# Projecting the keys of a linear attention in two 64-row tiles, by token parity

## The chip, the cores and the metric

The kernel runs on one core of one Trainium2 chip. The metric is the device time of one execution in microseconds, and for a kernel the median of its runs. Three runs before the change gave 900.4, 898.79 and 900.29 us: the median is 900.29 us. The engines are named as in the profile: PE (TensorE) for matmuls and PEld for its weight loads, DVE (VectorE), ACT (ScalarE), POOL (GpSimd), and SP, which issues most of the loads and stores.

## The reference

Three stages follow one another, all in float32. The first is an attention with features, for 4 batches, 8 heads, 576 tokens, 64 numbers per head and 128 features:

```python
def phi(x):
    proj = np.einsum('bhsd,df->bhsf', x, w_phi)
    proj = proj - np.max(np.abs(proj), axis=-1, keepdims=True)
    return np.concatenate([np.exp(proj), np.exp(-proj)], axis=-1)
q_p, k_p = (phi(q), phi(k))
kv = np.einsum('bhsf,bhsd->bhfd', k_p, v)
z = np.sum(k_p, axis=2)
num = np.einsum('bhsf,bhfd->bhsd', q_p, kv)
den = np.einsum('bhsf,bhf->bhs', q_p, z)[..., None] + 1e-06
```

Its result `num / den`, as 2304 rows of 512, goes through `((x @ w1) * (x @ w2)) @ w3 @ w_out`, and that through `g @ w_out` with `g = relu(x @ w_in)**2`.

## The kernel before

The attention works on pairs of heads: 16 pairs, four to a batch. Of a pair's 576 tokens, 512 are handled as four blocks of 128 (`C = 4`, `P = 128`), and the 64 left over, the tail, together with the tail of the next pair. Even pairs carry the work for the tails of two pairs, odd pairs don't, so that the pattern repeats after a double slot: an even and an odd pair.

For each pair PE transposes q and k into PSUM (`turn_q`, `turn_k`, line 350, tiles `pqt` and `pkt`; `turn_tails` makes `ptt`). Each transposed block is split into a high and a low part (`high_part`, line 353 on ACT; `low_part`, line 356 on DVE) with the tiles `qT`, `kT`, `tT`. Every product of two such values is made of three matmuls, high by high, low by high, high by low. The queries are projected by `project_sides` (line 436) into `pq`; the keys by `proj_k` (line 312), with a block of `kT` as the stationary operand and `wbd`, the feature weights of both heads in a block-diagonal layout, as the moving one. `project_k` is called for j = 0 and 1 (two PSUM banks `pk`, two token blocks each) and j = 2 (the tail). From `pk` DVE takes the largest absolute value (`peak_k`, line 411, tile `kmax`) and subtracts it (`less_k`, line 421, tile `kp`); ACT makes both exponentials (`exp_k`, line 428). `values` (line 511) multiplies them with v, `tail_values` (line 521) adds the tail; ACT copies the sum to `kv` (`keep_values`, line 529). For the queries, `max_q` and `max_qt` (line 451) find the maxima, `max_rows` (line 459) transposes them, `max_parts` (lines 466 to 469, tile `mh`) splits them, `send` moves them through a DMA into `mrow`, and `minus_q` (line 483) subtracts them in PSUM; then `exp_q` follows. One pair later `out` (lines 543 and 551) multiplies queries with `kv`, `keep` (line 559, tile `nd`) copies the result, `reciprocals` and `quotients` divide (DVE line 566, POOL line 578, tile `xd`); two pairs later `turn_x` (line 584) transposes the finished rows, and `keep_x` stores them.

Between these steps the weights of the first MLP are loaded and decoded (`w-1`, `w0`, `w1` and so on: a load on SP, `dy_...` on ACT at line 150, `dt_...` on DVE, additions on POOL).

The order of all this is written out by hand in four tables. `START` covers the first pairs and `END` the last ones from slot 13 on; in between a loop walks through `SLOT` for even and `ODD` for odd slots. An entry as `project_k0/5` runs a step for slot 5; each step has an offset, so that for slot t `turn_k` works on pair t + 1, `project_k` on pair t, `out` on pair t - 1 and `turn_x` on pair t - 2. The order of the entries is the order of the instructions on every engine: each engine works its own queue off in that order, and waits where an operand or a buffer is not ready. Of PSUM, three banks rotate (tag `t`) among `pkt`, `pqt`, `ptt`, the `pk` and `pkv`; `pq` and `po` are single.

Behind the attention, from about 188 us on, come the MLPs, which the change doesn't touch.

## Time and profile before

| what | value |
|---|---|
| median of three runs | 900.29 us |
| the profiled execution, its own time | 902.77 us |
| its span in the profile | 901.0 us |
| granted clock, mean over the span | 0.998 |
| PE busy | 887.2 us, 98% |
| PE weight loads busy | 773.6 us |
| DVE busy | 569.9 us, 63% |
| ACT busy | 412.1 us, 46% |
| POOL busy | 147.4 us, 16% |

Shares are of the whole span. Of the attention, some 188 us, the windows of 20 us show DVE and ACT much busier than that, at 15 to 17 us of 20 each, beside a PE of 18 to 20. Positions in the trace are microseconds from the start of the span. The profiled execution is one of its own and is 2.5 us above the median.

### The profile page before, as it was taken

What the parts mean: (1) busy time and instruction counts of PE and PEld (TensorE: products, weight loads), DVE (VectorE), ACT (ScalarE), POOL (GpSimd) and SP (SyncE); (2) the same over time, 40 slices, a digit from 0 to 9 for tenths busy, and PEclk for the clock granted to TensorE, in tenths of its full rate; (3) what the DMA queues carried; (4) which work ended last, traced back from release to release, by engine and by line L of the source; (5) the groups of instructions that cost most, each with busy time, mean ns of one, the idle gap of its engine ahead of it and who ended that gap; (6) DMA issues with size and microseconds to landing.
All of it is one profiled execution on the core that took longest, in us unless ns stands there. A gap on an engine that the chain in (4) does not pass through costs nothing.

```text
span 901.0 us, 16482 instructions
## 1 busy us (share of the span) xinstructions
PE 887.2 (98%) x6468; PEld 773.6 (86%) x6468; DVE 569.9 (63%) x1070; ACT 412.1 (46%) x787; POOL 147.4 (16%) x130
## 2 busy tenths in 40 slices
PE   8999999999999999999999999999999999999998
PEld 6888888778888888998888898989898998989896
DVE  6877777656766476567887865465745347643533
ACT  5888877754544545555565422232422123322211
POOL 3555655444212440000000000000000000000000
PEclk9999999999999999999999999999999999999999
DMA  6456565557343355758887898577586664684621
GB/s 172 138 164 179 149 189 162 136 131 172 94 140 94 118 164 164 260 167 293 298 289 281 312 398 317 176 269 256 176 315 204 246 227 148 236 325 157 227 99 71
DMA packets 120238, 182.72 MB, mean 203 GB/s; under 512 B 60320, under 2 KB 79584, under 8 KB 120160
## 3 DMA queue, kind: packets, MB, share of 16 engines
q1 hardware_dynamic: 119104, 180.84, 60.6%
q8 instruction: 51, 0.84, 0.4%
q10 hardware_dynamic: 1056, 0.82, 0.3%
q14 instruction: 27, 0.22, 0.1%
HBM read 140.54 MB, written 40.89 MB: 201 GB/s over the span
## 4 chain that ended last, share of the span: by engine, by line
PE 86%; ACT 4%; DMA 3%; DVE 3%; issue 1%; SPq 1%; POOL 1%; DVEq 0%; POOLq 0%; ACTq 0%
PE op L1319 22%; PE yp L1026 11%; PE pa L248 11%; PE pb L248 11%; PE ph_y L1283 8%; PE ph_x L1283 6%; PE ph_w L1283 6%; PE pf L953 5%; ACT kp L428 2%; DMA raw_w<-in_moe_w_dram 2%; PE pkv L511 1%; PE pq L436 1%; PE pk L312 1%; PE po L543 1%; ACT qp L490 1%
## 5 line engine op out<-in xcount | busy, mean ns | idle before, releaser
L1319 PE MATMUL op<-pair,r 128*128 128x512 f32 x864 | 202.9, 391 | 0.0
L1319 PEld LDWEIGHTS op<-pair,r 128*128 128x128 f32 x864 | 161.8, 188 | 32.2
L1026 PE MATMUL yp<-g,w3o 128*128 128x512 f32 (+1 forms) x480 | 105.1, 368 | 0.0
L1026 PEld LDWEIGHTS yp<-g,w3o 128*128 128x128 f32 x480 | 84.2, 189 | 14.9
L248 PE MATMUL pa<-c,w_w12a 128*128 128x512 f32 (+1 forms) x432 | 93.6, 366 | 0.0
L248 PE MATMUL pb<-c,w_w12b 128*128 128x512 f32 (+1 forms) x432 | 93.5, 366 | 0.0
L1283 PE MATMUL ph_y<-yf_t,pair 128*128 128x384 f32 x432 | 86.9, 335 | 0.0
L248 PEld LDWEIGHTS pa<-c,w_w12a 128*128 128x128 f32 x432 | 75.2, 189 | 13.1
L248 PEld LDWEIGHTS pb<-c,w_w12b 128*128 128x128 f32 x432 | 75.2, 189 | 13.1
L1283 PEld LDWEIGHTS ph_y<-yf_t,pair 128*128 128x128 f32 x432 | 76.1, 188 | 0.8 <-issue 0.4
L1370 DVE TENSOR_TENSOR u<-ph_y,m 128x384 f32<-128x384 f32 x24 | 13.4, 558 | 73.5 <-PE ph_y L1283 72.3
L1193 ACT ACTIVATE g<-g 128x512 fp32r<-128x512 f32 (+1 forms) x39 | 23.0, 590 | 78.4 <-DVE g L1191 78.4
L1283 PE MATMUL ph_x<-yf_b,pair 128*128 128x384 f32 x288 | 58.2, 337 | 0.0
L1191 DVE TENSOR_TENSOR g<-pb,a 128x512 f32<-128x512 f32 (+1 forms) x39 | 24.8, 636 | 51.9 <-PE pb L248 51.8
L1296 ACT ACTIVATE r<-m 128x384 fp32r<-128x384 f32 x43 | 22.6, 526 | 73.6 <-DVE m L1295 73.6
L1283 PEld LDWEIGHTS ph_x<-yf_b,pair 128*128 128x128 f32 x288 | 51.3, 188 | 1.9
L428 ACT ACTIVATE kp<-kp 128x512 f32<-128x512 f32 (+1 forms) x80 | 46.6, 589 | 7.6 <-DVE kp L421 6.2
L1366 ACT COPY m<-ph_x 128x384 f32<-128x384 f32 x24 | 11.5, 481 | 74.2 <-PE ph_x L1283 74.2
L953 PE MATMUL pf<-w_wo,w3T 128*128 128x512 f32 x192 | 45.0, 390 | 0.0
L953 PEld LDWEIGHTS pf<-w_wo,w3T 128*128 128x128 f32 x192 | 36.0, 188 | 7.5
L1297 DVE TENSOR_TENSOR r<-m,r 128x384 fp32r<-128x384 f32 x43 | 24.0, 558 | 25.4 <-ACT r L1296 25.4
L511 PEld LDWEIGHTS pkv<-vs,kp 128*64 128x64 f32 x1024 | 34.0, 143 | 6.4 <-ACT kp L428 3.4
(181 smaller groups left out, 1515.0 us busy)
## 6 DMA issues: line engine op xcount, KB each, us to landing
pair<-pair_hbm SPq DMA_DIRECT2D x144, 512.0 KB
pair_hbm<-w_w SPq DMA_DIRECT2D x32, 512.0 KB
raw_w<-in_moe_w_in_dram SPq DMA_DIRECT2D x16, 512.0 KB
raw_w<-in_moe_w_out_dram SPq DMA_DIRECT2D x16, 512.0 KB
pair_hbm<-v_w SPq DMA_DIRECT2D x16, 512.0 KB
raw_w<-in_moe_w_dram SPq DMA_DIRECT2D x56, 128.0 KB
x<-x_hbm SPq DMA_DIRECT2D x12, 512.0 KB
yi<-y_hbm SPq DMA_DIRECT2D x12, 384.0 KB
```

The source lines that it names most:

```text
L248: nc.tensor.matmul(ps[:, 0:n], a, c, start=kk + i == 0, stop=kk == KD - 1 and i == 2)
L428: nc.scalar.activation(z["kp", j][:, :, s, :], z["kp", j][:, :, 1, :], AF.Exp, scale=1.0 - 2.0 * s)
L511: nc.tensor.matmul(z["pkv"][h, s, j], z["kp", j][:, c, s, h], z["vs"][:, j, c, :], start=j + s + c == 0, stop=False, skip_group_check=True,)
L953: nc.tensor.matmul(pf, a, c, start=n == 0, stop=n == len(todo) - 1)
L1026: nc.tensor.matmul(blk.yp[i][:, 0:blk.n], a, d, start=c == blk.c0 and s == 0, stop=c == blk.c1 - 1 and s == 2)
L1191: nc.vector.tensor_tensor(out=g32[:, 0:n], in0=pb[:, 0:n], in1=a_sb[:, 0:n], op=ALU.mult)
L1193: nc.scalar.activation(g[:, 0, 0:n], g32[:, 0:n], AF.Copy)
L1283: nc.tensor.matmul(ps_, a, c, start=start and n == 0, stop=n == 5, skip_group_check=not start)
L1296: nc.scalar.activation(r[:, 0], h, AF.Copy)
L1297: nc.vector.tensor_tensor(out=r[:, 1], in0=h, in1=r[:, 0].bitcast(F32), op=ALU.subtract)
L1319: nc.tensor.matmul(z.ops[i], a, d, start=z.p + j + s == 0, stop=z.p == NP2 - 1 and j == 1 and s == 2)
L1370: nc.vector.tensor_tensor(out=u2, in0=y, in1=m1, op=ALU.add)
```

## The change

The keys are projected in two tiles of 64 rows each. Rows 0 to 63 of a transposed block hold the even tokens of a block of token pairs and rows 64 to 127 the odd ones. Each half is now the stationary operand of a matmul of its own, with the 64-row feature weights `wss` as the moving one, 128 columns in place of the 256 of `wbd`; even tokens go into one PSUM bank, odd tokens into another, and the two alternate from matmul to matmul. So there are 24 matmuls of 128x128 in place of 12 of 128x256 per pair. Both banks are one step, `project_k`; the tail keeps its form (`project_k2`). `peak_k`, `less_k` and `exp_k`, as code, stay as they are, but what 0 and 1 stand for is now the parity of the token and no longer a group of blocks; `values` picks its blocks accordingly, in the same number of matmuls. The four tables are written in another order. The diff of the tables, from which a line or two says little, is cut to its `ODD` part; the functions follow whole:

```diff
 ODD = """
-project_k0 peak_k0 project_q project_qt max_q tail_values< keep_values turn_x w1 keep_x max_qt turn_k w0 max_rows w1
-less_k0 project_k1 max_parts out turn_q peak_k1 high_k exp_k0 less_k1 exp_k1 keep turn_tails low_k values0 reciprocals
...
+project_k project_q project_qt tail_values< peak_k0 max_qt max_q keep_values w1 turn_x keep_x turn_k less_k0 max_rows
+w0 high_k turn_q out w1 max_parts exp_k0 send fetch_q fetch_k w-1 store_x peak_k1 less_k1 exp_k1 keep turn_tails
...
@@ -307,13 +306,6 @@
                 )
             return t
 
-        def proj_k(ps, at, kT, c):
-            for n, (a, b) in enumerate(passes((kT[:, 0], kT[:, 1]), (wbd[:, 0], wbd[:, 1]))):
-                nc.tensor.matmul(
-                    ps[:, at:at + 2 * F], a[:, c * P:(c + 1) * P], b.rearrange("p j f -> p (j f)"),
-                    start=n == 0, stop=n == 2,
-                )
-
         todo = [(b, pr) for b in range(B) for pr in range(NPR)]
         live = [{} for _ in todo]
         tails = {}
@@ -395,13 +387,25 @@
         def low_tail(z):
             low_part(z["tT"], z["ptt"][:, 0:2 * P])
 
-        def project_k(z, j):
-            z["pk", j] = ps = bank(f"pk_{z['nm']}_{j}")
-            if j < 2:
-                for g in range(2):
-                    proj_k(ps, g * 2 * F, z["kT"], 2 * j + g)
-            else:
-                proj_k(ps, 0, z["tT"][:, :, P:], 0)
+        def project_k(z):
+
+            at = [bank(f"pk_{z['nm']}_{u}") for u in range(2)]
+            for i in range(4):
+                for n, (a, b) in enumerate(((0, 0), (0, 1), (1, 0))):
+                    for u in range(2):
+                        h = slice(u * D, (u + 1) * D)
+                        nc.tensor.matmul(
+                            at[u][:, i * F:(i + 1) * F], z["kT"][h, a, i * P:(i + 1) * P], wss[h, b, :],
+                            start=n == 0, stop=n == 2,
+                        )
+            z["pk", 0], z["pk", 1] = at
+
+        def project_k_tails(z):
+            z["pk", 2] = ps = bank(f"pk_{z['nm']}_2")
+            for n, (a, b) in enumerate(passes((z["tT"][:, 0], z["tT"][:, 1]), (wbd[:, 0], wbd[:, 1]))):
+                nc.tensor.matmul(
+                    ps[:, 0:2 * F], a[:, P:], b.rearrange("p j f -> p (j f)"), start=n == 0, stop=n == 2
+                )
 
         def peak_k(z, j):
 
@@ -501,17 +505,18 @@
 
         halves_f = [slice(0, F // 2), slice(F // 2, F)]
 
-        def values(z, j):
-
-            if j == 0:
+        def values(z, u):
+
+            if u == 0:
                 z["pkv"] = bank(f"pkv_{z['nm']}")[:, 0:4 * (D + 1)].rearrange("p (s j d) -> p s j d", s=2, j=2)
-            for s in range(2):
-                for c in range(C):
-                    for h in halves_f:
-                        nc.tensor.matmul(
-                            z["pkv"][h, s, j], z["kp", j][:, c, s, h], z["vs"][:, j, c, :],
-                            start=j + s + c == 0, stop=False, skip_group_check=True,
-                        )
+            for j in range(2):
+                for s in range(2):
+                    for g in range(2):
+                        for h in halves_f:
+                            nc.tensor.matmul(
+                                z["pkv"][h, s, j], z["kp", u][:, 2 * j + g, s, h], z["vs"][:, j, 2 * g + u, :],
+                                start=u + j + s + g == 0, stop=False, skip_group_check=True,
+                            )
 
         def tail_values(z):
             pr = z["pr"]
@@ -708,8 +713,10 @@
         }
         for j in range(2):
             steps[f"values{j}"] = 0, lambda z, j=j: values(z, j)
+        steps["project_k"] = 0, project_k
+        steps["project_k2"] = 0, even(project_k_tails)
         for j in range(3):
-            for name, f in (("project_k", project_k), ("peak_k", peak_k), ("less_k", less_k), ("exp_k", exp_k)):
+            for name, f in (("peak_k", peak_k), ("less_k", less_k), ("exp_k", exp_k)):
                 steps[f"{name}{j}"] = 0, even(f, j) if j == 2 else lambda z, f=f, j=j: f(z, j)
 
 
```

The rows below show how that stands on three engines. `pk_1_0` and `pk_1_1` are the two banks of pair 1 of a batch, `pq_100` the queries, `pq_101` their tail and the row of maxima, `pkv_0` and `vt` the values of the pair before.

PE, the end of an even slot and the odd slot behind it, before:

```order
L511 MATMUL pkv_0_984<-vs_93,kp_0_1_982 64x65 x16
L312 MATMUL pk_1_0_1058<-wbd,kT_1_957 128x256 x6
L436 MATMUL pq_100<-qT_1_1016,wss 128x512 x6
L436 MATMUL pq_101<-tT_0_826,wss 128x128 x3
L521 MATMUL pkv_0_984<-vt_96,kp_0_2_1021 64x130 x4
L584 MATMUL po<-ident,xd_3_1018 128x128 x5
L350 MATMUL pkt_2_1092<-ident,km_2_1012 128x128 x4
L459 MATMUL pq_101<-ident,m_1_98 128x128
L312 MATMUL pk_1_1_1104<-wbd,kT_1_957 128x256 x6
L543 MATMUL po<-kv_0_1081,qp_0_1045 64x65 x32
L350 MATMUL pqt_2_1148<-ident,qm_2_1010 128x128 x4
```

The same place after the change (the two middle rows go on alternating, 24 in all):

```order
L516 MATMUL pkv_0_1061<-vs_93,kp_0_1_1050 64x65 x16
L397 MATMUL pk_1_0_1118<-wss,kT_1_974 128x128
L397 MATMUL pk_1_1_1119<-wss,kT_1_974 128x128
...
L440 MATMUL pq_100<-qT_1_1059,wss 128x512 x6
L440 MATMUL pq_101<-tT_0_871,wss 128x128 x3
L526 MATMUL pkv_0_1061<-vt_96,kp_0_2_1105 64x130 x4
L589 MATMUL po<-ident,xd_3_1099 128x128 x5
L342 MATMUL pkt_2_1171<-ident,km_2_1036 128x128 x4
L463 MATMUL pq_101<-ident,m_1_98 128x128
L342 MATMUL pqt_2_1184<-ident,qm_2_1034 128x128 x4
L548 MATMUL po<-kv_0_1161,qp_0_1102 64x65 x32
```

The second bank of `pk` has moved from behind the transposes of the keys to the front of the slot, ahead of `pq`, and the transposes of the queries (`pqt`) from behind the outputs (`po` from `kv` and `qp`) to ahead of them.

DVE, in an even slot, from the second reduction of the keys on, before:

```order
L411 TENSOR_REDUCE kmax_0_1_970<-pk_0_1_897 128x4
L466 TENSOR_REDUCE mh_0_976<-pq_101 48x32
L468 TENSOR_REDUCE m_0_978<-pq_101 48x32
L469 TENSOR_TENSOR mh_0_976<-m_0_978,mh_0_976 48x32
L356 TENSOR_TENSOR kT_1_957<-pkt_1_912,kT_1_957 128x512
L421 TENSOR_TENSOR kp_0_1_982<-pk_0_1_897,kmax_0_1_970 128x4x128
L566 TENSOR_SCALAR rc_3_1003<-nd_3_974 128x10
L569 RECIPROCAL rc_3_1003<-rc_3_1003 128x10
L411 TENSOR_REDUCE kmax_0_2_1006<-pk_0_2_964 128x2
L421 TENSOR_TENSOR kp_0_2_1021<-pk_0_2_964,kmax_0_2_1006 128x2x128
L152 TENSOR_SCALAR dt_wo_905<-dy_wo_904 128x512
L153 SCALAR_TENSOR_TENSOR dt_wo_905<-raw_wo_823,dt_wo_905 128x512
```

And after:

```order
L470 TENSOR_REDUCE mh_0_1025<-pq_101 48x32
L472 TENSOR_REDUCE m_0_1027<-pq_101 48x32
L473 TENSOR_TENSOR mh_0_1025<-m_0_1027,mh_0_1025 48x32
L415 TENSOR_REDUCE kmax_0_1_1030<-pk_0_1_938 128x4
L348 TENSOR_TENSOR kT_1_974<-pkt_1_967,kT_1_974 128x512
L425 TENSOR_TENSOR kp_0_1_1050<-pk_0_1_938,kmax_0_1_1030 128x4x128
L415 TENSOR_REDUCE kmax_0_2_1054<-pk_0_2_1019 128x2
L571 TENSOR_SCALAR rc_3_1056<-nd_3_1048 128x10
L574 RECIPROCAL rc_3_1056<-rc_3_1056 128x10
L151 TENSOR_SCALAR dt_wo_964<-dy_wo_963 128x512
L152 SCALAR_TENSOR_TENSOR dt_wo_964<-raw_wo_839,dt_wo_964 128x512
L425 TENSOR_TENSOR kp_0_2_1105<-pk_0_2_1019,kmax_0_2_1054 128x2x128
```

The parts of the maxima (`mh`) have moved ahead of the reduction `kmax_0_1`, the tail's reduction `kmax_0_2` ahead of the reciprocals, and the tail's difference `kp_0_2` behind the decoding of a weight.

ACT, at the end of the attention, slot 14 (`dy_w_0` decodes a part of w3, `nd_1` is the copy of the outputs), before:

```order
L173 ACTIVATE w_w12b_2744<-dt_w12b_2591 128x512
L353 ACTIVATE kT_3_2794<-pkt_3_2782 128x512
L150 ACTIVATE dy_w_0_2796<-raw_w_0_2675 128x512
L428 ACTIVATE kp_2_0_2780<-kp_2_0_2780 128x4x128 x2
L559 COPY nd_1_2850<-po 128x650
L428 ACTIVATE kp_2_1_2856<-kp_2_1_2856 128x4x128 x2
L353 ACTIVATE qT_3_2898<-pqt_3_2866 128x512
```

And after:

```order
L345 ACTIVATE kT_3_2973<-pkt_3_2968 128x512
L172 ACTIVATE w_w12b_2896<-dt_w12b_2775 128x512
L432 ACTIVATE kp_2_0_2966<-kp_2_0_2966 128x4x128 x2
L564 COPY nd_1_3027<-po 128x650
L149 ACTIVATE dy_w_0_3033<-raw_w_0_2876 128x512
L432 ACTIVATE kp_2_1_3036<-kp_2_1_3036 128x4x128 x2
L345 ACTIVATE qT_3_3052<-pqt_3_3046 128x512
```

The decoding `dy_w_0` has moved from ahead of the first exponentials and the copy `nd_1` to behind them. At the start of the kernel, likewise, the transposes of the first tail (`turn_tails/-1`) now stand ahead of the first `project_q/0` in the table. On SP the sends and loads keep their order among one another but for the first few; on POOL the order is the same.

## Rows read from the trace of the kernel before

**Rows 1.** The page, part 4: the chain that ended last, shares by engine.
```profile
PE 86%; ACT 4%; DMA 3%; DVE 3%; issue 1%; SPq 1%; POOL 1%; DVEq 0%; POOLq 0%; ACTq 0%
```

**Rows 2.** Timeline of PE: start, length, operation [idle before <-releaser].
```profile
90.95 0.66 PE L584 MATMUL po<-ident,xd 128*128 128x128 f32 x4 [1.03 <-POOL xd L578]
...
100.89 0.98 PE L312 MATMUL pk<-wbd,kT 128*128 128x256 f32 x6
...
101.92 0.97 PE L436 MATMUL pq<-qT,wss 64*128 64x512 f32 x6
...
103.10 0.66 PE L521 MATMUL pkv<-vt,kp 128*64 128x130 f32 x8
...
111.62 0.55 PE L584 MATMUL po<-ident,xd 128*128 128x128 f32 x3
```

**Rows 3.** The same view, at three other places.
```profile
37.59 0.98 PE L312 MATMUL pk<-wbd,kT 128*128 128x256 f32 x6
...
133.40 0.66 PE L584 MATMUL po<-ident,xd 128*128 128x128 f32 x4 [0.78 <-POOL xd L578]
...
143.34 0.77 PE L584 MATMUL po<-ident,xd 128*128 128x128 f32 x5
```

**Rows 4.** Chain of waits, us 83 to 92: start, length, what.
```profile
79.96 4.60 DMA raw_wo<-in_moe_w_out_dram
```

**Rows 5.** Chain of waits, us 98 to 113.
```profile
103.81 0.38 ACT kv L529
...
106.97 1.16 ACT kp L428 x2
```

**Rows 6.** Weight loads: line 312's by source (min/median/max ns), then two timeline rows.
```profile
L312 PEld LDWEIGHTS pk<-wbd,kT x192: 186/188/221, 7.2 to 171.7; 128*128 128x128 f32 x192
...
91.53 0.30 PEld L436 LDWEIGHTS pq<-qT,wss 64*128 64x128 f32 x4 [0.17 <-ACT qpt L497]
...
92.70 1.47 PEld L312 LDWEIGHTS pk<-wbd,kT 128*128 128x128 f32 x12
```

**Rows 7.** Timeline of DVE, even slot, then odd slot.
```profile
93.99 0.65 DVE L411 TENSOR_REDUCE kmax<-pk 128x4 f32<-128x512 f32 x1
...
98.27 0.17 DVE L566 TENSOR_SCALAR rc<-nd 128x10 f32<-128x10 f32 x1 [0.51 <-ACT nd L559]
...
100.97 0.68 DVE L356 TENSOR_TENSOR qT<-pqt,qT 128x512 fp32r<-128x512 f32 x1
...
103.00 1.45 DVE L451 TRANSPOSE_TENSOR_REDUCE m<-pq 128x32 f32<-128x1024 f32 x2 [0.40 <-ACT kp L428]
...
104.37 0.65 DVE L421 TENSOR_TENSOR kp<-pk,kmax 128x512 f32<-128x512 f32 x1
...
106.76 0.69 DVE L421 TENSOR_TENSOR kp<-pk,kmax 128x512 f32<-128x512 f32 x1
```

**Rows 8.** Timeline of all engines at the start.
```profile
7.93 0.42 DVE L356 TENSOR_TENSOR tT<-ptt,tT 128x256 fp32r<-128x256 f32 x1 [0.93 <-ACT tT L353]
...
14.34 0.49 PE L483 MATMUL pq<-mrow,minus 2*128 2x512 f32 x3 [0.67 <-DMA mrow<-mh]
```

**Rows 9.** Timeline of all engines, pair 14, at the end of the attention.
```profile
160.42 0.45 PE L551 MATMUL po<-kv,qpt 128*64 128x65 f32 x8
...
160.52 0.70 ACT L150 ACTIVATE dy_w<-raw_w 128x512 f32<-128x512 f32 x1 [1.53 <-DMA raw_w<-in_moe_w_dram]
...
162.14 0.50 PE L483 MATMUL pq<-mrow,minus 2*128 2x512 f32 x3 [0.17 <-DMA mrow<-mh]
...
162.31 0.68 ACT L559 COPY nd<-po 128x650 f32<-128x650 f32 x1
...
164.34 3.47 PE L511 MATMUL pkv<-vs,kp 128*64 128x65 f32 x60 [1.70 <-DVE kT L356]
```

**Rows 10.** Windows of 2 us: busy time (instructions) of PE, PEld, DVE, ACT, POOL; clock; DMA.
```profile
164.00:166.00 2.00, 1.66 (x32) 1.69 (x34) 1.97 (x5) 2.00 (x4) 1.92 (x3) 0.61 1.24 260
166.00:168.00 2.00, 2.00 (x39) 1.90 (x36) 0.96 (x3) 1.55 (x5) 1.92 (x2) 0.54 0.34 56
```

More of the change, by code (lines that the diff above doesn't have):

```diff
@@ L41 @@
[L41 to L43 removed]
+fetch_k/0 warm6/0 turn_q/-1 turn_k/-1 high_q/-1 low_q/-1 turn_tails/-1 project_q/0 high_k/-1 low_k/-1 keep_tails/-1
+project_k/0 low_tail/-1 project_qt/0 max_q/0 project_k2/0 max_qt/0 peak_k0/0 max_rows/0 less_k0/0 exp_k0/0 max_parts/0
@@ L44 @@
+w0/2 exp_qt/2 exp_k2/2 load_v/2
 """.split()
 SLOT = """
[L46 to L49 removed]
+keep_values turn_x project_q keep_x project_qt max_q project_k w0 max_qt turn_k peak_k0 high_k less_k0 max_rows out
@@ L73 @@
-last/16 w1/17 w1/16 w0/16 w0/17 w0/17 w0/16 w0/17 prefetch/16
+turn_x/13 project_q/13 project_qt/13 tail_values/12 w1/13 keep_values/13 project_k/13 keep_x/13 max_q/13 max_qt/13
+turn_k/13 w0/13 max_rows/13 peak_k0/13 w1/13 less_k0/13 max_parts/13 exp_k0/13 high_k/13 send/13 fetch_q/13 fetch_k/13
+store_x/13 out/13 peak_k1/13 keep/13 less_k1/13 turn_q/13 low_k/13 exp_k1/13 turn_tails/13 values0/13 reciprocals/13
+quotients/13 minus_q/13 high_q/13 w-1/13 keep_tails/13 x_load/13 exp_q0/13 low_tail/13 low_q/13 w0/13 exp_q1/13 w0/13
@@ new lines @@
+exp_qt/13 w0/13 values1/13 tail_values/13 load_v/13 project_k/14 project_q/14 keep_values/14 project_qt/14 turn_x/14
+keep_x/14 max_q/14 max_qt/14 peak_k0/14 less_k0/14 turn_k/14 high_k/14 w1/14 max_rows/14 max_parts/14 peak_k1/14 w1/14
+out/14 exp_k0/14 keep/14 send/14 w-1/14 w0/14 less_k1/14 exp_k1/14 reciprocals/14 quotients/14 turn_q/14 low_k/14
+high_q/14 project_k2/14 peak_k2/14 minus_q/14 values0/14 exp_q0/14 exp_q1/14 w0/14 w0/14 exp_qt/14 less_k2/14
+values1/14 low_q/14 turn_x/15 exp_k2/14 late/15 project_q/15 project_qt/15 tail_values/14 max_q/15 max_qt/15 w0/14
```

55 lines of the change are left out of this document (21 added, 34 removed).

## The prediction

> **What bounds the kernel now.** I read the page first: the chain that ended last is TensorE (PE) for 86% of the span [rows 1]. That share hides two regimes. From about 188 us on the MLPs keep PE full, and the change touches none of their instructions. In the attention before it, PE, VectorE (DVE) and ScalarE (ACT) hand work to one another, so there I went on to the timeline of one double slot (an even and an odd head pair), to the chain of waits in it, and to the two ends of the attention. The reader should look for two things: by how much a double slot exceeds the clean 20.67 us, and which wait ends last where it does.
>
> From one even pair's transposes of the finished rows (line 584, x4) to the next is 111.62 - 90.95 = 20.67 us in a double at whose end PE doesn't wait for them [rows 2]; the next one, from 111.62 to 133.40, at whose end it waits 0.78 us for POOL's xd, takes 21.78, and the one before it ends with a wait of 1.03 [rows 2, 3]. The loop over pairs writes five doubles, each beginning with an odd slot's pk: from 37.59 to 143.34, 105.75 us against 5 x 20.67 = 103.35 [rows 2, 3]. So 2.4 us of waits are in them. In the double that ends at 90.95 the root is a load: issued at 79.96, raw_wo landed 4.60 us later, and ACT's dy_wo, which needs it, stands ahead of kT, the exponentials and nd in ACT's order, so that xd came late [rows 4].
>
> A clean double is no looser. ACT's copy of kv at 103.81 starts a chain ACT, DVE, POOL that runs without a gap of note to the next transposes at 111.62: 7.81 us, whatever PE does meanwhile [rows 2, 5].
>
> **The multiplications.** Twelve matmuls 128x256 per pair become twenty-four 128x128 with 64 rows, in couples, one on either half of the rows. Before, a weight load takes 0.188 us and twelve span 1.47, so they stand (1.47 - 0.19)/11 = 0.116 apart and a pair costs 1.40 us. Four 64-row loads of the q projection span 0.30: two at a time, and the next two (0.30 - 0.19) = 0.11 later [rows 6]. So 24 matmuls are 12 x 0.11 = 1.32 us: 0.08 less per pair, 1.3 us over 16 pairs if PE were the limit everywhere. It isn't; I count it inside the terms below. Bounds: if a couple's two loads went one after the other, 24 x 0.11 = 2.64 (+1.24 a pair); if the matmuls and not the loads set the pace, half of 1.40, 0.70 (-0.70 a pair). I take 1.32, the nearest row in shape.
>
> The Trainium skill has a rule for either end. "TensorEngine Tiling (Array Packing)", section "Theoretical Speedup", holds out up to twice the speed for 64 rows; by that, 0.70 a pair. "TensorE: Matmul & The Clock Gate", section "LDWEIGHTS (loading the stationary operand)", sets a load's time by the columns of the stationary operand and not by its rows, an estimated 107 ns for 128: 1.28 a pair. The trace's 0.11 sides with the second, which is why the first is only the third rival.
>
> **The even slot of the loop.** PE begins pk at 92.70 as before, and ends its 24 near 92.70 + 1.32 + 0.12 = 94.14, both banks together, so DVE's first kmax starts 0.15 later than its 93.99 [rows 6, 7]. The tail's kmax (0.42 us there) now stands ahead of the reciprocals, where DVE sat idle 0.51 us for nd [rows 7]. So DVE's low part of qT, which ended at 100.97 + 0.68 = 101.65, or 10.70 after the slot's start, ends at 10.70 + 0.15 - 0.51 = 10.34. max_parts goes ahead of the second kmax, a reduction of about 0.65 us as at 93.99; less the 0.15, max_parts, the send and the loads behind it on SP come some 0.45 us earlier.
>
> **The odd slot.** This is where I expect the loss. Before, only the first bank of pk stood ahead of pq: 100.89 (9.94 after the start), and pq at 101.92 (10.97) [rows 2]. Now both banks stand ahead of pq, and the second needs a bank that frees when DVE's low part of qT has read it, at 10.34 by the last paragraph. The two banks alternate, so PE stops at the second matmul until about 10.38; behind it stand, in PE's order, pk, pq, the tail values, the transposes. 10.38 + 1.32 = 11.70 for pq; 103.10 - 101.92 = 1.18 later the tail values: 12.88 against 12.15 before, +0.73. ACT's kv waits for them, and its 7.81 us hang on that [rows 2, 5]. A second count goes by DVE: max_qt now precedes max_q and both wait for the later pq, so the 1.45 us of the two maxima run from about 12.95 to 14.4 (before: 103.00, or 12.05, to 13.4); from there less_k0, max_parts, kmax and less_k1 took 106.76 + 0.69 - 104.37 = 3.08 us, to 17.5, where ACT took up exp_k1 halfway in the piece at 106.97, at 16.6 [rows 5, 7]: +0.9. I take +0.8 a double. PE's own work would allow about 21.1 to 21.3, since pqt, moved ahead of the outputs, waits some 0.5 us for less_k0 (14.4 + 0.65 = 15.1): inside the 21.47.
>
> Five doubles: 5 x 21.47 = 107.35 against 105.75, or **+1.6 us**. The 2.4 us of waits are thereby covered: the load is issued about 0.45 earlier and ACT asks for it 0.73 later, together 1.18 against the longest wait of 1.03 [rows 2, 3].
>
> **The start.** The tail's transposes move ahead of the q projection. Before, DVE idled 0.93 us for the tail's high part and its low part stood ahead of max_q; the send of the maxima, further down that line, kept PE waiting 0.67 us at 14.34 [rows 8]. Half a microsecond of shift is there to be had and 0.67 is the most that PE gets back. **-0.5 us**, bounds 0 and -0.7.
>
> **The end, pair 14.** Before, ACT's dy_w waited 1.53 us for a load and stood ahead of exp_k0 and nd. nd began at 162.31 though PE's outputs were done at 160.42 + 0.45 = 160.87; DVE's kT hung on it, and PE waited 1.70 us until 164.34 [rows 9]. Right after this wait the granted clock is 0.61 and 0.54 for two stretches of 2 us with PE busy 1.66 and 2.00 [rows 10], between the two levels of 1.2 and 2.4 GHz: 0.39 x 1.66 + 0.46 x 2.00 = 1.6 us lost. Now dy_w stands behind nd. nd can begin near 160.9, 1.4 us earlier, and the values with it, near 162.9, when PE has just finished the minus step at 162.14 + 0.50 = 162.64. With 0.3 us of idle in place of 1.70 I expect the clock to stay up. **-1.4 - 1.6 = -3.0 us**; bounds: 0 if another wait takes over, -3.3 if all of it goes.
>
> **The sum.** +1.6 - 0.5 - 3.0 = -1.9 us. The profiled execution took 902.77 us (span 901.0), so 900.9 for it; the median of the runs is 900.29, 2.5 below, so **898.4 us**.
>
> **Rivals.**
> First, slower: the odd slot pays for everything in a row. If the wait for less_k0 ahead of pqt (about 0.5) adds to the 0.9 in place of lying beside it, and the loads are asked for by a send that is itself late in the odd slot, the old waits stay. 5 x 1.4 = +7.0 - 3.5 = +3.5: 903.8 us. For it: all engines are in order and three queues meet in this slot. Against it: PE's outputs lie 1 us ahead of ACT's nd. It decides once every double takes about 22.0 us.
> Second, no change: the load for pair 14 is issued at a send that comes later, lands some 1.3 us later and makes ACT's dy_w hold exp_k1 and the q side instead, and the clock falls all the same. The end gives -0.3 only: +1.6 - 0.5 - 0.3 = +0.8: 901.1 us. For it: ACT was held by that load until 160.52 already [rows 9]; against it: nothing PE needs first stands behind it any more.
> Third, faster: pairs at 0.70 us. Both counts of the odd slot shrink by 0.62, a double is about 20.87, the loop 5 x 0.2 - 2.4 = -1.4; the last two pairs, where PE is short of nothing else, give 1.2; with start and end -6.1: 894.2 us. Against it: the spacing of 0.11 in both kinds of load [rows 6].
> Last, couples loaded one after the other: 16 x 1.24, near 920 us; the four-load row speaks against it.
>
> **How the numbers follow.** Forecast 45% (its own range 896.8 to 900.2), first rival 20%, second 20%, third 13%, the last 2%. From 894.0 to 903.8 some 8 in 10 are held, with a part of the outer rivals beyond either end. No change means within 0.2%, 1.8 us. The forecast lies just at that edge: half of it counts as faster (0.23) and nearly half as same (0.20); the second rival is mostly same (0.14), the third all faster; the first mostly slower. Faster 0.40, same 0.35, slower 0.25.
>
> **What would show it.** In the changed profile: pk as 24 matmuls spanning about 1.4 us; in odd slots an idle time of PE of about 0.5 us before pk that ends with DVE's qT; doubles of about 21.4 to 21.5, all alike, with no wait for a load; ACT's dy_w behind nd near 160, PE's wait there under 0.5 us and a granted clock of 1.0 after it. The forecast is wrong if doubles stay below 21 (the odd slot had slack that I don't see), or if the clock still falls at the end.

## The result, and the profile after

The changed kernel takes 910.35 us (median of four runs, 906.01 to 914.21) against 900.06 us: the ratio is 1.0116, with an interval of 1.0066 to 1.0165. Forecast was 898.4, with 894.0 to 903.8 as the range. The change costs about 10 us, and the runs, which lay within 2 us of one another, now spread over 8.

The profiled execution after is the fastest of the four, 906.01 us; the one before, 902.77, lies 2.7 us above its median. So the two traces differ by 3.2 us only, and the medians by 10. Here is the page of after, with its span, its busy times and the shares of the chain that ended last [rows 1]:

```profile
span 904.2 us, 16862 instructions
...
PE 886.9 (98%) x6660; PEld 771.2 (85%) x6660; DVE 571.5 (63%) x1070; ACT 411.7 (46%) x787; POOL 147.2 (16%) x130
...
PE 87%; DVE 4%; ACT 4%; DMA 2%; issue 1%; POOL 1%; SPq 0%; ACTq 0%; DVEq 0%; POOLq 0%
```

PE has the same work to do. To find where the time went I cut the two traces at two marks: the first odd slot's pk [rows 3] and the transposes of slot 13, with which the hand-written end begins. In the timeline of PE after:

```profile
38.47 0.29 PE L397 MATMUL pk<-wss,kT 64*128 64x128 f32 x1
```
```profile
149.53 0.66 PE L589 MATMUL po<-ident,xd 128*128 128x128 f32 x4
```

Before, the marks are 37.59 and 143.34 in a span of 901.0; after, 38.47 and 149.53 in one of 904.2. So the start is 0.9 us longer, the loop takes 111.06 in place of 105.75 (+5.3), and what follows takes 754.7 in place of 757.7 (-3.0). Forecast were -0.5, +1.6 and -3.0. These are differences of two single executions; a second trace of the kernel before, further down, does not bear out the -3.0.

What PE waits for between 38 and 150 us, first after, then before (us in total, times, longest):

```profile
PE pqt L342 <- PE pk L406: 2.2, 3, 0.7
PE po L589 <- POOL xd L583: 2.1, 5, 1.1
PE pqt L342 <- DVE kp L425: 1.0, 4, 0.2
PE pk L397 <- DVE qT L348: 0.4, 2, 0.2
```
```profile
PE po L584 <- POOL xd L578: 2.1, 3, 1.0
PE pq L436 <- ACT qp L490: 0.3, 1, 0.3
```

The wait for xd, which the prediction had as covered, is the same 2.1 us. New is the wait ahead of pqt, three times 0.72. One double slot after, in PE's timeline; it takes 95.45 - 73.22 = 22.23 us against the clean 20.67 [rows 2]:

```profile
73.22 0.65 PE L589 MATMUL po<-ident,xd 128*128 128x128 f32 x4 [0.19 <-POOL xd L583]
...
80.84 0.63 PE L342 MATMUL pqt<-ident,qm 128*128 128x128 f32 x4 [0.72 <-PE pk L406]
...
84.04 1.92 PE L397 MATMUL pk<-wss,kT 64*128 64x128 f32 x24
85.69 1.02 PE L440 MATMUL pq<-qT,wss 64*128 64x512 f32 x6
...
86.92 0.66 PE L526 MATMUL pkv<-vt,kp 128*64 128x130 f32 x8
...
95.45 0.66 PE L589 MATMUL po<-ident,xd 128*128 128x128 f32 x4 [0.20 <-POOL xd L583]
```

The even half is late by 10.82 - 9.94 = 0.88 us when the odd slot's pk begins (84.04 - 73.22), and the odd half takes 11.41 against 10.73. The odd half was forecast. The even half was not. PE's pk of the tail is named as the releaser of pqt, but it had ended at 80.12; what pqt waits for is a PSUM bank, which VectorE frees when its low part of kT is done, at 80.07 + 0.67 = 80.74. Two rows of after, VectorE and GpSimd, show why that is late:

```profile
78.27 1.27 DVE L473 TENSOR_TENSOR mh<-m,mh 48x32 fp32r<-48x32 f32 x1
```
```profile
78.21 1.29 POOL L174 TENSOR_TENSOR w_wo<-dt_wo,w_wo 128x512 fp32r<-128x512 f32 x1 [2.06 <-ACT w_wo L172]
```

And the same two steps in a clean double before:

```profile
54.08 0.19 DVE L469 TENSOR_TENSOR mh<-m,mh 48x32 fp32r<-48x32 f32 x1
```
```profile
52.94 1.28 POOL L175 TENSOR_TENSOR w_wo<-dt_wo,w_wo 128x512 fp32r<-128x512 f32 x1 [1.36 <-ACT w_wo L173]
```

The subtraction of 48x32 numbers that ends max_parts takes 0.19 us; after, it takes 1.27. It began 0.06 us after a subtraction of GpSimd and ended 0.04 us after it. Everything behind it on VectorE (kT, kp, the tail, qT) is 1.08 us later. Three of the loop's five even slots show it (56.05, 78.27 and 143.75). In the double from 95.45 the subtraction began ahead of GpSimd's, at 100.50 against 100.65, took 0.18, and the double takes 21.14. So a hit costs 22.22 - 21.14 = 1.08 us.

The double from 116.59 is not hit either, 0.18 us at 121.64, and takes 22.12 us all the same. There ScalarE stands 3.07 us for the load of a weight:

```profile
116.59 0.66 PE L589 MATMUL po<-ident,xd 128*128 128x128 f32 x4 [0.19 <-POOL xd L583]
...
138.71 0.66 PE L589 MATMUL po<-ident,xd 128*128 128x128 f32 x4 [0.45 <-POOL xd L583]
```
```profile
121.02 0.70 ACT L149 ACTIVATE dy_w12a<-raw_w12a 128x512 f32<-128x512 f32 x1 [3.07 <-DMA raw_w12a<-in_moe_w_dram]
```

So four of the five even slots are late, three by the collision and one by a load.

Two things in the description of the kernel before need a correction: wbd holds the feature weights twice, for the two tokens of a pair that lie in the two halves of the rows, not for two heads; and before the change a bank of pk belongs to a head, with two blocks of token pairs.

### The profile page after: what moved, and what is told of

The parts are those of the page before. It is cut to its first block, busy times and chain, and to the rows that moved or that the text cites. A ratio compares the mean times of both kernels' runs of the same rounds, so it can differ in the third digit from the quotient of the medians.

```text
span 904.2 us, 16862 instructions
## 1 busy us (share of the span) xinstructions
PE 886.9 (98%) x6660; PEld 771.2 (85%) x6660; DVE 571.5 (63%) x1070; ACT 411.7 (46%) x787; POOL 147.2 (16%) x130
## 4 chain that ended last, share of the span: by engine, by line
PE 87%; DVE 4%; ACT 4%; DMA 2%; issue 1%; POOL 1%; SPq 0%; ACTq 0%; DVEq 0%; POOLq 0%
PE op L1326 22%; PE yp L1033 11%; PE pb L247 11%; PE pa L247 11%; PE ph_y L1290 8%; PE ph_x L1290 6%; PE ph_w L1290 6%; PE pf L960 5%; PE pk L397 2%; ACT kp L432 2%; PE pq L440 2%; PE pkv L516 1%; DVE kmax L415 1%; DVE kp L425 1%; POOL xd L583 1%
## 5 line engine op out<-in xcount | busy, mean ns | idle before, releaser
L152 DVE SCALAR_TENSOR_TENSOR dt_w<-raw_w,dt_w 128x512 int32<-128x512 int32 x48 | 36.3, 756 | 1.6
```

The lines of the kernel that those rows point to most:

```text
L152: nc.vector.scalar_tensor_tensor(out=t, in0=hi, scalar=-(1 << 31), in1=t, op0=ALU.bitwise_and, op1=ALU.bitwise_or)
```

## The experiments

Times are medians; each ratio is to runs of the kernel before on the same chip. Of the kernel before there were medians of 898.95 to 899.64 us in these comparisons.

**The spread, and VectorE against GpSimd.** First the changed kernel once more, unaltered.

> The changed kernel unaltered, for its spread (906.0 to 914.2 us so far, before: 898.8 to 900.4). Theory A (VectorE against GpSimd): in even slots the small subtraction that ends max_parts, line 473, begins within 0.1 us of GpSimd's subtraction for a weight, line 174, and where it begins second it lasts until that has ended, 1.27 us in place of 0.18. By A the number of even slots of the loop with a long line 473 (3 of 5 in the first trace) changes from run to run; five would be some 2 us more than three, none 3 us less. Rival B: the delay of the even slots is the order of PE (the tail's pk ahead of pqt), is the same in each double, and the spread has another origin, such as loads.

Measured: 909.21 us, 906.12 to 911.68, ratio 1.0108 (1.0076 to 1.0139). In its trace other doubles are hit: VectorE at 100.41, which was spared the first time, and not at 143.97.

```profile
100.41 1.27 DVE L473 TENSOR_TENSOR mh<-m,mh 48x32 fp32r<-48x32 f32 x1
```
```profile
100.35 1.29 POOL L174 TENSOR_TENSOR w_wo<-dt_wo,w_wo 128x512 fp32r<-128x512 f32 x1 [2.06 <-ACT w_wo L172]
```
```profile
143.97 0.18 DVE L473 TENSOR_TENSOR mh<-m,mh 48x32 fp32r<-48x32 f32 x1
```

Three of five again, but not the same three, and each hit double takes 22.22 or 22.23 us. So which slots are hit is a matter of the single execution, as A has it. The number changes, too: a later trace of the changed kernel with another order at its start (911.26 us, under "The start") has all five hit, and its loop takes 114.14 us against 111.06 and 111.10 with three.

The whole spread does not come from this. Two of the four runs here have a mean granted clock of 0.999 and 0.998 (906.12 and 908.37 us) and two of 0.994 (910.04 and 911.68 us); 0.006 of a span of 908 us is an estimated 5.4 us. In the first four runs the clock says nothing: 914.21 us had 0.999.

The next kernel moves both w1 in front of high_k:

```diff
-keep_values turn_x project_q keep_x project_qt max_q project_k w0 max_qt turn_k peak_k0 high_k less_k0 max_rows out
-project_k2 w1 w1 max_parts peak_k1 send fetch_q fetch_k fetch_tails w-1 store_x low_k turn_q exp_k0 keep less_k1
+keep_values turn_x project_q keep_x project_qt max_q project_k w0 w1 w1 max_qt turn_k peak_k0 high_k less_k0 max_rows
+out project_k2 max_parts peak_k1 send fetch_q fetch_k fetch_tails w-1 store_x low_k turn_q exp_k0 keep less_k1 exp_k1
```

> The changed kernel with one edit in SLOT: both w1 (ScalarE's high part of a weight and GpSimd's subtraction) directly behind w0, ahead of high_k, as in the kernel before. GpSimd's subtraction then starts some 0.7 us earlier and is over when VectorE reaches line 473. A: line 473 takes 0.2 us in every even slot, PE's wait of 0.72 us for pqt goes, doubles take 21.1 to 21.4 in place of 22.2, the loop 4 us less than in the first trace, the time 902 to 904 us, and the spread is under 2.5 us. B: doubles stay at 22.2 us and the time at 906 to 914.

Measured: 904.68 us, 903.14 to 905.53, ratio 1.0057 (1.0035 to 1.0080): 4.5 us less than the kernel after in the same comparison, with a spread of 2.4. GpSimd is done at 77.20 and VectorE starts at 77.30:

```profile
75.92 1.28 POOL L173 TENSOR_TENSOR w_wo<-dt_wo,w_wo 128x512 fp32r<-128x512 f32 x1 [0.74 <-ACT w_wo L171]
```
```profile
77.30 0.18 DVE L472 TENSOR_TENSOR mh<-m,mh 48x32 fp32r<-48x32 f32 x1
```

Doubles take 21.15, 21.46, 21.66 and 22.80 us; the last still has one hit, of 1.15 us, where ScalarE waited 2.24 us for a weight's load, so that GpSimd came late again:

```profile
118.98 0.67 ACT L148 ACTIVATE dy_w12a<-raw_w12a 128x512 f32<-128x512 f32 x1 [2.24 <-DMA raw_w12a<-in_moe_w_dram]
```

A holds, and B, PE's order, falls: the order was not touched. The 4.5 us are a difference of medians. The loop of this one trace, with a hit and waits for loads left in it, takes 109.94 us, only 1.1 less than in the traces with three hits; and the mean clocks of the two sets of runs differ (0.999 to 0.994 there, 0.998 to 0.996 here). So the collision's own share is known by its 1.08 us a hit, 3.2 us with three and 5.4 with five, and not to the last tenth.

The same the other way round, in the kernel before: both w1 behind high_k.

```diff
-turn_x keep_values project_q project_qt project_k0 max_q max_qt keep_x project_k1 w0 w1 w1 peak_k0 max_rows turn_k out
-high_k turn_q project_k2 less_k0 peak_k1 exp_k0 keep max_parts low_k less_k1 values0 exp_k1 reciprocals peak_k2 send
+turn_x keep_values project_q project_qt project_k0 max_q max_qt keep_x project_k1 w0 peak_k0 max_rows turn_k out
+high_k w1 w1 turn_q project_k2 less_k0 peak_k1 exp_k0 keep max_parts low_k less_k1 values0 exp_k1 reciprocals peak_k2
```

> The kernel before with one edit in SLOT: both w1 behind high_k, which puts GpSimd's subtraction 0.7 us later in even slots. Theory A (VectorE's small subtraction lasts until GpSimd's ends where they meet): GpSimd runs from about 5.1 to 6.4 us after the even transposes, line 469 begins at 5.44 and lasts about 1.0 us in place of 0.18 in most even slots, doubles grow by 0.6 to 0.9 us, the time to 902 to 904 us. If ScalarE's order alone mattered, or nothing, 898 to 900 us and line 469 stays at 0.2.

Measured: 901.39 us, ratio 1.0022 (1.0008 to 1.0035). Every even slot from 54 to 140 us is hit, for 1.11 us:

```profile
75.58 1.11 DVE L469 TENSOR_TENSOR mh<-m,mh 48x32 fp32r<-48x32 f32 x1
```
```profile
75.36 1.28 POOL L175 TENSOR_TENSOR w_wo<-dt_wo,w_wo 128x512 fp32r<-128x512 f32 x1 [2.28 <-ACT w_wo L173]
```

Clean doubles take 21.16 us, 0.5 more and not 0.6 to 0.9. So the same collision costs the old order less than half of what it costs the new one, 0.5 against 1.08 us a double, where max_parts stands ahead of more of VectorE's work and pqt waits for kT.

**Tiles and order apart.** The new multiplications in the old order: project_k0 and project_k1 become the one step, at the place of the first.

```diff
-project_k0 peak_k0 project_q project_qt max_q tail_values< keep_values turn_x w1 keep_x max_qt turn_k w0 max_rows w1
-less_k0 project_k1 max_parts out turn_q peak_k1 high_k exp_k0 less_k1 exp_k1 keep turn_tails low_k values0 reciprocals
+project_k peak_k0 project_q project_qt max_q tail_values< keep_values turn_x w1 keep_x max_qt turn_k w0 max_rows w1
+less_k0 max_parts out turn_q peak_k1 high_k exp_k0 less_k1 exp_k1 keep turn_tails low_k values0 reciprocals
```

> The kernel before with the new multiplications alone (two tiles of 64 rows, features by token parity), its four tables kept but for one thing that the tiles force: both banks are one step, which stands where the first of the two stood. By the account of the odd slot (kv waits for pq, which now waits for both banks), doubles are 21.2 to 21.5 in place of 20.7, no even slot is late by line 473's wait, and the time is 901 to 903 us. If the tiles as such are slow (loads of a couple one after the other), 915 us or more; if they are no loss, 898 to 900.

Measured: 909.67 us, ratio 1.0109 (1.0079 to 1.0140). A miss by 7 us, and not through slow couples. PE's rows:

```profile
29.78 1.55 PE L398 MATMUL pk<-wss,kT 64*128 64x128 f32 x23 [1.03 <-DVE tT L349]
```
```profile
62.20 0.32 PE L398 MATMUL pk<-wss,kT 64*128 64x128 f32 x1
62.95 1.55 PE L398 MATMUL pk<-wss,kT 64*128 64x128 f32 x23 [0.43 <-DVE qT L349]
64.23 1.02 PE L441 MATMUL pq<-qT,wss 64*128 64x512 f32 x6
```
```profile
163.66 1.55 PE L398 MATMUL pk<-wss,kT 64*128 64x128 f32 x23 [0.99 <-DVE tT L349]
```

Two matmuls, one a bank, can't both start until both banks are free. At 62.20 one matmul runs, and the other 23 stand behind the second bank's wait for qT; at 29.78 and 163.66 it is the tail's low part, for 1.0 us. The couples themselves are as fast as counted: 23 matmuls span 1.55 us and one takes 0.27, so they stand (1.55 - 0.27)/22 = 0.058 apart, half of the 0.11 between loads. PE's waits ahead of pk add up to 2.0 us for the tail's low part and 1.3 for qT in this trace; doubles take 21.67 to 22.86 us, with two even slots hit, for 0.73 and 0.99 us. How the whole loss divides among these was not tested.

The new order with the old multiplications, both banks in one step:

```diff
+        def project_k(z):
+
+            for j in range(2):
+                z["pk", j] = bank(f"pk_{z['nm']}_{j}")
+                for g in range(2):
+                    proj_k(z["pk", j], g * 2 * F, z["kT"], 2 * j + g)
```

> The changed kernel's four tables with the multiplications of before (128 rows, 256 columns, one bank a head), both banks in the one step project_k. If the order is what costs, and the tiles only their 0.1 us a pair, then 907 to 912 us, doubles of 22.2 us where line 473's subtraction meets GpSimd's, and a pause in odd slots shorter than before since the first bank doesn't wait for VectorE. If the tiles cost more than half of the loss, under 904.

Measured: 904.06 us, ratio 1.0053 (1.0037 to 1.0068): below what was expected. No even slot is hit; VectorE is 0.2 us earlier there, where the first bank ends before the second, and begins ahead of GpSimd:

```profile
55.94 0.18 DVE L474 TENSOR_TENSOR mh<-m,mh 48x32 fp32r<-48x32 f32 x1
```
```profile
56.21 1.29 POOL L174 TENSOR_TENSOR w_wo<-dt_wo,w_wo 128x512 fp32r<-128x512 f32 x1 [2.17 <-ACT w_wo L172]
```

So the tiles cost in the old order, and the new order costs without the tiles. With the collision mostly moved away the new order has ratios of 1.0057 with the tiles and 1.0053 without them: there the tiles show neither gain nor loss. As for the collision, three of five even slots are hit in the first two traces of tiles and new order together, two with the tiles alone, none with the new order alone. The kernel before has one in its first trace:

```profile
117.05 0.99 DVE L469 TENSOR_TENSOR mh<-m,mh 48x32 fp32r<-48x32 f32 x1
```

Doubles take 21.28 us (51.10 to 72.38), with PE's queries behind both banks:

```profile
51.10 0.66 PE L589 MATMUL po<-ident,xd 128*128 128x128 f32 x4 [0.69 <-POOL xd L583]
...
61.08 1.68 PE L392 MATMUL pk<-wbd,kT 128*128 128x256 f32 x12
62.69 0.96 PE L441 MATMUL pq<-qT,wss 64*128 64x512 f32 x6
...
63.86 0.66 PE L526 MATMUL pkv<-vt,kp 128*64 128x130 f32 x8
...
72.38 0.33 PE L589 MATMUL po<-ident,xd 128*128 128x128 f32 x1 [0.19 <-POOL xd L583]
```

**The odd slot.** The same kernel with the two banks as two steps again in ODD:

```diff
-project_k project_q project_qt tail_values< peak_k0 max_qt max_q keep_values w1 turn_x keep_x turn_k less_k0 max_rows
-w0 high_k turn_q out w1 max_parts exp_k0 send fetch_q fetch_k w-1 store_x peak_k1 less_k1 exp_k1 keep turn_tails
+project_k0 project_q project_qt tail_values< peak_k0 max_qt max_q keep_values w1 turn_x keep_x turn_k less_k0 max_rows
+project_k1 w0 high_k turn_q out w1 max_parts exp_k0 send fetch_q fetch_k w-1 store_x peak_k1 less_k1 exp_k1 keep
```

> The changed tables with the multiplications of before, but in ODD the two banks are two steps again: the first ahead of the queries, the second behind max_rows, ahead of the outputs, as in the kernel before. With both banks ahead of the queries the same kernel had doubles of 21.28 us, kv began 12.8 us into them, and the time was 904.1. If the odd slot's loss is that kv waits for pq and pq for both banks, kv begins 0.6 to 0.7 us earlier, doubles are 20.6 to 20.8, the loop about 2.5 us less, the time 901 to 902 us. If another part of the order is the cause, doubles stay at 21.2.

Measured: 901.01 us, ratio 1.0025 (1.0015 to 1.0036). That is 3.0 us less by the medians and 2.5 by the ratios, since the two kernels were compared with other runs of the kernel before, on other chips. Doubles take 20.71 to 20.74 us, but for the last with 21.11:

```profile
71.68 0.66 PE L588 MATMUL po<-ident,xd 128*128 128x128 f32 x4
...
92.42 0.66 PE L588 MATMUL po<-ident,xd 128*128 128x128 f32 x4
```

So the second bank ahead of the queries makes the odd slot's loss, as the prediction had it, about 0.56 us a double.

**The end.** In the kernel before, the decoding of a part of w3 moved behind nd:

```diff
-project_k1/14 high_k/14 w0/14 max_rows/14 max_parts/14 peak_k1/14 w1/14 out/14 exp_k0/14 keep/14 send/14 w-1/14
+project_k1/14 high_k/14 max_rows/14 max_parts/14 peak_k1/14 w1/14 out/14 exp_k0/14 keep/14 send/14 w-1/14 w0/14
```

> The kernel before with one edit in END: the first w0/14 (ScalarE's dy_w) behind exp_k0, keep, send and w-1 of slot 14, as in the changed kernel. If the prediction's third term is right, PE's wait of 1.70 us at 164.3 and the fall of the granted clock after it go: -3.0 us, about 897 us. The rival of the prediction: the load's wait moves to exp_k1 and the q side, -0.3 us.

Measured: 898.47 us, ratio 0.9993 (0.9983 to 1.0004). Its trace shows what was forecast: PE waits 0.23 us where it waited 1.70, and the clock stays at 1.00 [rows 9, 10].

```profile
161.88 1.33 PE L511 MATMUL pkv<-vs,kp 128*64 128x65 f32 x38 [0.23 <-DVE kT L356]
```

But the median hardly moves. Hence a second trace of the kernel before:

> The kernel before, unaltered, for a second trace of it. The first one (902.77 us) is above every other run of this kernel (897.6 to 901.7), and the kernel with the end's edit alone measured only 0.5 us less than it, not 3.0. If the fall of the granted clock behind PE's wait for pair 14 is a matter of the single execution, this trace shows a clock of 1.0 between 160 and 170 us, or a shorter wait there, and about 899 us. If it is in every execution, it shows the same 0.5 to 0.6 again, and the edit's gain was lost elsewhere.

Measured: 900.01 us, and there the clock does not fall either. Windows of 4 us of this second trace, and of the first:

```profile
164.00:168.00 4.00, 4.00 (x80) 3.42 (x74) 2.38 (x4) 3.87 (x9) 3.43 (x3) 1.00 0.78 166
```
```profile
164.00:168.00 4.00, 3.66 (x65) 3.59 (x66) 2.93 (x6) 3.55 (x8) 3.83 (x4) 0.57 0.79 158
```

In this trace PE waits 0.91 us there, for the row of the maxima and not for kT, and the granted clock stays:

```profile
163.13 0.50 PE L483 MATMUL pq<-mrow,minus 2*128 2x512 f32 x3 [0.91 <-DMA mrow<-mh]
```

Behind the mark of slot 13 this second trace takes 898.2 - 143.59 = 754.6 us, as long as the trace of after, without any edit:

```profile
143.59 0.77 PE L584 MATMUL po<-ident,xd 128*128 128x128 f32 x5
```

Of the sixteen traces of this study, the first one is the only one with a fall in this window; two others have one from 168 us on.

**The start.** Two edits on the tail's transposes, one in either kernel. In the changed kernel they go back behind the first project_q:

```diff
-fetch_k/0 warm6/0 turn_q/-1 turn_k/-1 high_q/-1 low_q/-1 turn_tails/-1 project_q/0 high_k/-1 low_k/-1 keep_tails/-1
+fetch_k/0 warm6/0 turn_q/-1 turn_k/-1 high_q/-1 low_q/-1 project_q/0 turn_tails/-1 high_k/-1 low_k/-1 keep_tails/-1
```

> The changed kernel with one edit in START: the tail's transposes behind the first project_q again, as before. In the first trace PE waits at 6.66 for the load of the tail's queries (landed 6.52 us) with pq queued behind it, which starts at 7.25 in place of 5.38. If that made the start late, pq starts at 5.4, the first send comes 0.5 us earlier than 11.72, and the first odd slot's pk near 37.6 in place of 38.5. If the start is bound by the order behind the first send, pk stays at 38.3 to 38.6.

Measured: 910.39 us, ratio 1.0116 (1.0088 to 1.0144), no change. pq did start earlier, at 5.76, but in this trace the granted clock was 0.67 and then 0.50, the lower of its two levels, from 12 to 20 us, so the first odd slot says nothing. In the kernel before they go forward:

```diff
-warm6/0 fetch_k/0 turn_q/-1 turn_k/-1 high_q/-1 low_q/-1 project_q/0 high_k/-1 turn_tails/-1 keep_tails/-1 low_k/-1
+warm6/0 fetch_k/0 turn_q/-1 turn_k/-1 high_q/-1 low_q/-1 turn_tails/-1 project_q/0 high_k/-1 keep_tails/-1 low_k/-1
```

> The kernel before with one edit in START: the tail's transposes ahead of the first project_q, as the changed kernel has them. The prediction counted this at -0.5 us. By the traces of the changed kernel PE waits there until the tail's queries have landed at 6.5 us, with pq behind: the first pq at 7.1 to 7.3 in place of 5.4, the first send 0.3 to 0.5 us later, the time +0.5 to +1.0 us. If the prediction's account held, pq's tail and the send come earlier and the time falls by 0.5.

Measured: 898.67 us, ratio 0.9996 (0.9985 to 1.0007): nothing, neither the gain of the prediction nor the loss expected here. The profiled execution is the slowest of the ten, 901.15 us. The wait is there, 0.71 us for the load, with pq behind it:

```profile
6.52 0.45 PE L350 MATMUL ptt<-ident,qtl 128*128 128x128 f32 x1 [0.71 <-DMA qtl<-in_q_dram]
...
7.16 1.65 PE L436 MATMUL pq<-qT,wss 64*128 64x512 f32 x6
```

Then the changed START table alone in the kernel before, of which two places show the kind of edit:

```diff
-warm6/0 fetch_k/0 turn_q/-1 turn_k/-1 high_q/-1 low_q/-1 project_q/0 high_k/-1 turn_tails/-1 keep_tails/-1 low_k/-1
-project_k0/0 low_tail/-1 project_qt/0 project_k2/0 max_q/0 max_qt/0 peak_k0/0 less_k0/0 project_k1/0 exp_k0/0
...
+fetch_k/0 warm6/0 turn_q/-1 turn_k/-1 high_q/-1 low_q/-1 turn_tails/-1 project_q/0 high_k/-1 low_k/-1 keep_tails/-1
+project_k0/0 project_k1/0 low_tail/-1 project_qt/0 max_q/0 project_k2/0 max_qt/0 peak_k0/0 max_rows/0 less_k0/0
...
```

And this table with a bank of pk ahead of the queries in slots 1 and 2 (here parts of two lines, for slot 2):

```diff
-tail_values/1 low_tail/1 project_q/2 project_k0/2 project_k1/2 keep_values/2
+tail_values/1 low_tail/1 project_k0/2 project_q/2 keep_values/2 max_q/2
```

> The kernel before with the changed START table alone (multiplications of before; both steps of project_k side by side where the changed table has its one step). In every kernel with that table the first transposes of finished rows came 1.0 to 2.5 us later than in the kernel before. If the table is the cause, they come at 31 us in place of 29.4 and the time is 900.5 to 901.5 us. If it was the tiles or the single execution, 899 to 900.

> The same START, but in slots 1 and 2 a bank of pk stands ahead of the queries again, as in the kernel before, and the other behind them. If the start is late because pq stands first in these slots and waits for ScalarE's exponentials (0.44 and 0.36 us in the first trace) with nothing ahead of it, the first of these waits goes and the time is 0.8 to 1.2 us below that of start_alone. If the tail's transposes, which wait for their load, are the cause, the two times are equal.

Measured: 903.08 us, ratio 1.0041 (1.0025 to 1.0057), and 902.49 us, ratio 1.0039 (1.0028 to 1.0051). So the START table costs about 3.7 us by itself (2.2 to 5.1). Moving the tail's transposes alone cost nothing, and giving the keys their place in slots 1 and 2 back changed the median by 0.6 us, which the two intervals don't tell from nothing: the cause within the table stays open. The kernel of "The odd slot" has this table too, with nearly all else of the new order, and is only 2.3 us above the kernel before (1.3 to 3.2). The transposes of slot 2's finished rows come at 32.02 us in place of 29.4, with the queries' tail behind both banks at 9.68 (8.12 before). That is where I would look next; it was not tried.

**Faster than both.** The kernel before, with the end's edit and w-1 as the first entry of SLOT and ODD:

```diff
-turn_x keep_values project_q project_qt project_k0 max_q max_qt keep_x project_k1 w0 w1 w1 peak_k0 max_rows turn_k out
...
-fetch_q fetch_k fetch_tails w-1 store_x high_q quotients less_k2 minus_q values1 w0 w0 exp_q0 exp_q1 w0 exp_qt exp_k2
...
+w-1 turn_x keep_values project_q project_qt project_k0 max_q max_qt keep_x project_k1 w0 w1 w1 peak_k0 max_rows turn_k
...
+send fetch_q fetch_k fetch_tails store_x high_q quotients less_k2 minus_q values1 w0 w0 exp_q0 exp_q1 w0 exp_qt exp_k2
```

> The kernel before with the end's edit (dy_w behind nd in slot 14) and one more in SLOT and ODD: w-1, the load of the next weight, first in the slot in place of behind the send and the fetches. The waits of the loop's doubles for a load (2.4 us in the first trace) should go if the load is what comes late: doubles of 20.7 us throughout, 896 to 897 us. If the early load holds up the small transfer of the maxima instead, PE waits for mrow in every slot and the time is 900 us or more.

Measured: 897.64 us (896.11 to 898.44), ratio 0.9979 (0.9969 to 0.9990). Doubles take 20.79, 20.65, 20.67 and 20.67 us; PE's wait for xd is gone from its list of waits, that for the row of maxima is 1.8 us in four places of the attention, one of them in the loop. This is the fastest version, without the tiles.

The changed kernel with three repairs, in SLOT (and w-1 likewise in ODD) and in START as shown above:

```diff
-keep_values turn_x project_q keep_x project_qt max_q project_k w0 max_qt turn_k peak_k0 high_k less_k0 max_rows out
-project_k2 w1 w1 max_parts peak_k1 send fetch_q fetch_k fetch_tails w-1 store_x low_k turn_q exp_k0 keep less_k1
+w-1 keep_values turn_x project_q keep_x project_qt max_q project_k w0 w1 w1 max_qt turn_k peak_k0 high_k less_k0
+max_rows out project_k2 max_parts peak_k1 send fetch_q fetch_k fetch_tails store_x low_k turn_q exp_k0 keep less_k1
```

> The changed kernel with the tiles kept and three edits: both w1 ahead of high_k in SLOT, the tail's transposes behind the first project_q in START, and w-1 first in SLOT and ODD. Left are the odd slot's wait of pq for both banks (0.6 to 0.8 us a double, some 3.5 us) and the rest of the start: 901 to 903 us, against 904.7 with the first edit alone. If what remains lies in the tiles themselves, no better than 904.

Measured: 902.60 us (900.77 to 907.54), ratio 1.0043 (1.0028 to 1.0058). Doubles take 21.13 or 21.14 us, all alike and none hit. Of the 3.9 us that are left against the kernel before, the odd slot makes 5 x 0.47 = 2.4; that the rest is the start is a guess by subtraction. The runs spread over 6.8 us without a hit in the trace, and the three slowest (904.39 to 907.54) have mean clocks of 0.994 to 0.996 where the three fastest have 0.998 to 1.0. In the trace, the slowest run, the clock is low near the start:

```profile
16.00:20.00 4.00, 4.00 (x70) 3.88 (x70) 1.23 (x3) 2.02 (x3) 2.69 (x2) 0.50 0.16 65
```

PE was busy 0.98 of the 2 us from 10 and 1.17 of the 2 us from 12 before it; the first trace of after has 0.98 and 1.16 there, and a clock of 1.00 throughout. Of the five traces with both the tiles and the changed START table, three have such a fall between 10 and 21 us; of the other eleven, none. What brings it about was not tested.

## Why the prediction was wrong

*The even slot: the step that failed.* "So DVE's low part of qT ... ends at 10.34" took every operation of VectorE at its duration in the clean trace. The change put max_parts 0.4 us earlier, which the prediction counted, and both w1 behind high_k in SLOT, which it has no term for: ScalarE's w_wo, and with it GpSimd's subtraction, came 0.7 us later, though the order on POOL is the same. The two subtractions then begin within 0.06 us of one another. The low part of qT ended at 83.67 + 0.67 - 73.22 = 11.12; in the double from 95.45, which is not hit, at 104.83 + 0.68 - 95.45 = 10.06, better than forecast. Where neither the collision nor a load comes in, doubles are 21.13 to 21.15 us, less than the forecast 21.47. The edit that moves the collision away gave 4.5 us of the 10. Rows of before had it already: 0.99 us of this operation at 117.05, in the double of 21.78 us that the prediction put down to the wait for xd, and in odd slots 0.57 at 105.56, which it used inside the 3.08 us and did not ask about. "SBUF — State Buffer", section "Who interferes with whom", in the Trainium skill has the rule: a VectorE instruction with two inputs in SBUF and a GpSimd instruction that reads SBUF exclude each other, and the one that issues first keeps what they share until it has ended. The trace agrees, 1.27 us against 0.18.

*The odd slot: right, a little large.* Both banks ahead of the queries, kv later, the chain behind it as long as before: from kv at 87.63 to the transposes at 95.45 it is 7.82 us, and 7.81 was said. Forecast 0.8 us a double, measured 0.68 in a hit double of the first trace, 0.56 with the old multiplications and 0.47 in the kernel with three repairs. The pause of PE inside pk, forecast at 0.5 us, is 0.21 and stands in two slots only.

*The loads: not covered.* "The 2.4 us of waits are thereby covered" went by a load issued 0.45 us earlier and asked for 0.73 later. ScalarE still stood 3.07 us for one, at 121.02, and PE's wait for xd is 2.1 us as before. With w-1 at the front of the slot the late doubles are gone, in the kernel before (20.65 to 20.79 us) and in the changed one with three repairs (21.13 or 21.14).

*What the tiles do: half right.* Couples run side by side, at 0.058 us a matmul, near the 0.055 of the forecast, and neither bound came true. That two banks must be free at once I used only for the odd slot. With the tiles in the old order, 9.8 us slower, this wait stands at six places, 3.3 us of PE's idle time in the trace; the rest of the 9.8 was not taken apart.

*The end: right in the trace, by luck, and wrong in the sum.* The -3.0 us came out in the difference of the two traces. But the second trace of the kernel before takes the same 754.6 us for this stretch without the edit, as its clock doesn't fall and its wait is another, and the median of the edit alone shows 0.5 us (-0.4 to 1.5 by the interval 0.9983 to 1.0004). The prediction subtracted them from the median after saying that the profiled execution lay 2.5 us above it. Those 2.5 us were in good part this very fall, 1.6 by the prediction's own estimate.

*The start: wrong in sign.* Not -0.5 us; +0.9 in the trace, about +3.7 (2.2 to 5.1) for the table alone. The step "half a microsecond of shift is there to be had" asked what waits for the tail's transposes and not what they wait for, their own load, with pq queued behind them. That wait is shown; that it makes the time is not, since moving these transposes alone changed no median. The cause within the table stays open.

*The sum in hindsight.* By the ratios, from kernel to kernel: the new order with the banks as two steps in ODD costs 2.3 us, both banks ahead of the queries 2.5 more, the tiles 0.4, which is inside the noise, and the collision 4.6. That makes 9.7, as the last ratio must; the first medians differ by 10.3. The 2.3 are not taken apart: the START table alone measured 3.7, with intervals that overlap. The first rival, "slower", gave 903.8 by another road, the loads; its mark, doubles of about 22.0 us, came true in three doubles by the collision and in one by a load.
